# A gated linear attention with a PReLU network: the opening as one written sequence of small pieces, and state products ahead of off-diagonal ones

## The chip, the cores and the metric

The kernel runs on one core of one Trainium2 chip. Five engines run their own instruction streams and meet at semaphores: TensorE (PE; PEld is its weight load), VectorE (DVE), ScalarE (ACT), GpSimd (POOL) and SyncE (SP, which here only issues DMAs). The metric is the device time of one execution in microseconds, as the median over runs. All data are float32, but for the two weight matrices, which arrive as 64-bit floats and are turned into 32 bits on the chip.

## The reference

```python
# q, k, v, f_logit: (batch 4, heads 8, seq 768, dim 48)
f = 1.0 / (1.0 + np.exp(-f_logit))
for t in range(S):
    state = f[:, :, t, :, None] * state + np.einsum('bhd,bhe->bhde', k[:, :, t], v[:, :, t])
    y[:, :, t] = np.einsum('bhd,bhde->bhe', q[:, :, t], state)
x = y.transpose(0, 2, 1, 3).reshape(3072, 384)
h = x @ w_in                                   # w_in: 384 x 2048
g = np.maximum(h, 0.0) + alpha * np.minimum(h, 0.0)
out = g @ w_out                                # w_out: 2048 x 384
```

## The kernel before

The recurrence is cut into six chunks of 128 positions. A step is one chunk of two batch entries (eight heads each), so there are 12 steps: step n is the entry pair n % 2 and the chunk n // 2. Steps 0 and 1 have chunk 0, with an empty state and cheaper level products. Each step has four parts, written as generators that yield after a piece of work:

- `prepare` (P): loads of f, q, k, v (step 0 on SP's queue, the others on POOL's); the sigmoid and copies on ACT; on DVE the lagged products (L287 to L294), two scans (L317, L319), the level products (`us`) and the scaled queries and keys (`q3`, `kh`, `ks`); state queries copied into A (L419, ACT).
- `carry` (O): off-diagonal products `off` on PE (L444, and for chunk 0 the half products, L454) with ACT copies into A and `ad`; for chunk 0 the keys' transposes `pk`; then the state products `pd` (L484) and the first half of the state update, `moved(0)`.
- `attend` (S): for each of the two entries the scores `raw` (L520) and `qu` (L535) on PE, and masked copies of them into `ad` on DVE (L526, L541, L557); the diagonal blocks from `ad` to A (L563, eight copies, ACT); the outputs `py` (L574); `moved(1)`; the copy of `py` to `y` (ACT) and the change of layout to `xT`, in step 0 by products with `dense` (L592), later by ten DMAs on SP's, ACT's and POOL's queues.
- `network` (n): eight groups of the first layer `ph` (L618, six products of 256 columns), for each a Relu on ACT (L623) and two `gate` instructions on DVE (L625). The second layer is plain in step 0's network (`po`, L638), and in the others has seven half-size products in place of eight (L657), fed by sums of gates (L702) and of parts of w_out (L721).

The weights come in 16 pieces of 767 KB on SP's queue; ACT splits each (two instructions), and DVE combines them (L234). Piece f of w_in is what group f of step 0's network reads.

PE, DVE and ACT run in the order in which the program is written; a scheduler places POOL's and SP's instructions. That order is spelled out in letters, `FIRST` for the first four steps and `USUAL` for the others (Q is P of the next step, n the network of the step before). Ahead of all, 52 small products into a bank `idle` (L736) run on PE.

Of the kernel before, what the change touches and what calls it, by code (L numbers as in the profile page):

```python
# [17 lines left out]
C = 128  # L18
DB = 32
# [7 lines left out]
IDLE = 52  # L27
# [3 lines left out]
FIRST = (  # L31
        "P5 a2 P a O w S w a w a2 S Q S O S w Q2 S Q2 S w",
        "a2 w2 n O b w n b2 S P v2 n2 S b v Q n b n O S2 v n b v n Q2 b v Q b n S v2 W Q W S n2 W n",
        "n S P n2 S W n W n O Q n3 O S Q n S Q n Q S2 Q n3",
        "S n3 P S Q S n O n O n4 Q S Q S Q n S Q n Q n2",
)
USUAL = "S n2 S n2 O2 n Q n3 Q n Q S3 n Q S n Q n Q n"

def flat(first, usual, steps=12):
    out = []  # L40
    left = {}
    for n in range(steps + 1):
        for key in (first[n] if n < len(first) else usual).split():
            for _ in range(int(key[1:] or 1)):
                k = key[0]
                if k in "awbvW":
                    out.append((k,))
                else:
                    m = n - 1 if k == "n" else n + 1 if k == "Q" else n
                    k = "P" if k == "Q" else k  # L50
                    if 0 <= m < steps:
                        out.append((k, m))
    return out

# [4 lines left out]
def kernel(  # L59
# [12 lines left out]

# [31 lines left out]
    psn = ctx.enter_context(tc.tile_pool(name="psn", bufs=4, space=bass.MemoryType.PSUM))  # L120

    def pair(name):
        return psa.tile([128, 2, 512], F32, tag="pair", name=name)

    def bank(name):
        return psn.tile([128, 512], F32, tag="net", name=name)
# [35 lines left out]
    nc.gpsimd.memset(mquad, 0.0)  # L162
    for m in range(1, NB):
        lo = UO[m] + (4 if m == 1 else 0)
        n = NB - m
        nc.gpsimd.tensor_copy(mquad[:, lo:lo + 4 * n].rearrange("p (i r) -> p i r", r=4),
                              inq[:, 0:n].unsqueeze(2).broadcast_to((128, n, 4)))
    mhalf = const.tile([128, VW], F32, tag="mhalf", name="mhalf")
    nc.gpsimd.memset(mhalf, 0.0)
    for half in range(2):  # L170
        for m in range(1, NQ):
            n = NQ - m
            lo = 16 * half + 4 if m == 1 else VO[m] + 4 * n * half
            nc.gpsimd.tensor_copy(mhalf[:, lo:lo + 4 * n].rearrange("p (i r) -> p i r", r=4),
                                  inq[:, NQ * half:NQ * half + n].unsqueeze(2).broadcast_to((128, n, 4)))
# [7 lines left out]
    make_identity(nc, ident)  # L183
    nc.gpsimd.tensor_scalar(om, om, -1.0, 1.0, ALU.mult, ALU.add)


    dense = work.tile([128, DM], F32, tag="o", name="dense")
    nc.gpsimd.memset(dense, 0.0)
    for par in range(2):
        nc.gpsimd.tensor_copy(dense[:, (2 + par) * D:(3 + par) * D], ident[:, 64 * par:64 * par + D])  # L190

    def load_weights(dst, src, name):

        rows_ = NK if dst is w_in_sb else 1
        pieces_ = dst.shape[1] * dst.shape[2] // WP
        if rows_ == 1:
            dst = dst.rearrange("p a n -> p (a n)").unsqueeze(1)
        width = WP // rows_
        words = src.rearrange("p (a n) -> p a n", a=rows_).bitcast(I16)
        got = {}  # L210

        def of(n):
            return dst[:, :, n * width:(n + 1) * width]

        def by_row(t):
            return t.rearrange("p (a n) -> p a n", a=rows_)

        def upper(n):
            raw = stage.tile([128, WP, 4], I16, tag="raw", name=f"{name}_raw{n}", bufs=RAWS)
            nc.sync.dma_start(out=raw.rearrange("p (a n) four -> p a (n four)", a=rows_)[:, :, 0:4 * width - 1],  # L220
                              in_=words[:, :, 4 * n * width + 1:4 * (n + 1) * width])

            lead = stage.tile([128, WP], F16, tag="lead", name=f"{name}_lead{n}", bufs=LEADS)
            nc.scalar.activation(lead, raw[:, :, 2].bitcast(BF16), AF.Copy, scale=0.5)
            nc.scalar.activation(as_int(n, I32), by_row(raw.bitcast(U32)[:, :, 0]), AF.Copy, scale=2.0 ** -13)
            got[n] = lead

        def as_int(n, dtype):
            t = of(n).bitcast(dtype)
            return t if dtype is I32 else t.rearrange("p a (n two) -> p a n two", two=2)[:, :, :, 1]  # L230

        def both(n):
            t = by_row(got.pop(n).bitcast(I16))
            nc.vector.tensor_tensor(as_int(n, I16), as_int(n, I16), t, ALU.add)  # L234

        def uppers():
            for n in range(pieces_):
                upper(n)
                yield

        def rests():
            for n in range(pieces_):
                both(n)
                yield

        return uppers(), rests()
# [11 lines left out]
    def prepare(bp, c, x):  # L258

        i = f"{bp}_{c}"  # L260
        b0 = U * bp
        loads = nc.gpsimd if bp or c else nc.sync

        def load(name, src, bufs=2):
            t = work.tile([128, W], F32, tag=name, name=f"{name}_{i}", bufs=bufs)
            loads.dma_start(out=t.rearrange("p (u x) -> p u x", u=U),
                              in_=src[b0:b0 + U, c].rearrange("u p h t -> p u (h t)"))
            return t

        f = quads(load("f", fT, 1))  # L270
        q = load("q", qT, 1)
        k = x["k"] = load("k", kT, 1)

        for cc in range(NC2):
            t_, _ = halves(cc)
            loads.dma_start(out=vs[bp][t_, cc, :, 0:DM], in_=v[b0:b0 + U, c, t_].rearrange("u t d -> t u d"))


        nc.scalar.activation(f, f, AF.Sigmoid)
        nc.scalar.copy(kr[:, :, 2:3], f[:, :, 3:4])  # L280
        qdv = [qd[:, :, QO[d]:QO[d] + NB * (4 - d)].rearrange("p g (i r) -> p g i r", r=4 - d) for d in range(4)]
        nc.scalar.copy(qd[:, :, 0:DB], q.rearrange("p (g t) -> p g t", t=DB))  # L282
        fq = fs[:, 0:NS - 1].rearrange("p (g i) -> p g i", i=NB + 1)[:, :, 1:NB + 1]
        by32 = "p (g i) r -> p g (i r)"

        def lagged(d):
            nc.vector.tensor_tensor(qdv[d], qdv[d - 1][:, :, :, 1:5 - d],  # L287
                                    f[:, :, 1:5 - d].rearrange("p (g i) r -> p g i r", i=NB), ALU.mult)

        nc.vector.tensor_tensor(kr[:, :, 1:2], f[:, :, 2:3], f[:, :, 3:4], ALU.mult)  # L290
        lagged(1)
        nc.vector.tensor_tensor(kr[:, :, 0:1], f[:, :, 1:2], kr[:, :, 1:2], ALU.mult)
        lagged(2)
        nc.vector.tensor_tensor(fq, f[:, :, 0:1].rearrange(by32, i=NB), kr[:, :, 0:1].rearrange(by32, i=NB), ALU.mult)  # L294
        lagged(3)
        yield

        ps = work.tile([128, NS], F32, tag="ps", name=f"ps_{i}", bufs=1)  # L300
        ut = work.tile([128, G * UW], F32, tag="us", name=f"us_{i}", bufs=1)
        if c:
            us = ut.rearrange("p (g t) -> p g t", g=G)
        else:

            at = (0, VW, VW + 16, VW + 16 + DB, VW + 16 + DB + NB)
            us, q16, k16, g16 = (ut[:, G * lo:G * hi].rearrange("p (g t) -> p g t", g=G) for lo, hi in zip(at, at[1:]))
            nc.gpsimd.memset(k16[:, :, 16:DB], 0.0)
            nc.gpsimd.memset(g16[:, :, 3:5], 1.0)
            x["q16"], x["k16"] = q16, k16  # L310
        x["us"] = us
        q4 = us[:, :, 0:DB].rearrange("p g (i r) -> p g i r", r=4)
        for r in range(4):
            nc.scalar.copy(q4[:, :, :, r], qdv[r][:, :, :, 0])
        if not c:
            nc.scalar.copy(g16[:, :, 2:6:3], fq[:, :, 3:5])
        nc.vector.tensor_tensor_scan(ps, fs, ones, 0.0, ALU.mult, ALU.add)  # L317
        ss = work.tile([128, NS], F32, tag="ss", name=f"ss_{i}", bufs=1)
        nc.vector.tensor_tensor_scan(ss[:, ::-1], fs[:, ::-1], ones[:, ::-1], 0.0, ALU.mult, ALU.add)  # L319
        yield  # L320
        nc.vector.tensor_tensor(q4, q4, f[:, :, 0:1].rearrange("p (g i) o -> p g i o", i=NB)
                                .broadcast_to((128, G, NB, 4)), ALU.mult)
        pre = ps[:, 0:NS - 1].rearrange("p (g i) -> p g i", i=NB + 1)
        suf = ss[:, 1:NS].rearrange("p (g i) -> p g i", i=NB + 1)[:, :, 1:NB + 1]

        def earlier(m):

# [471 lines left out]
```

## Time and profile before

| What | Value |
|---|---|
| Median of 3 runs (lowest, highest) | 622.01 us (621.87, 624.6) |
| The profiled execution's span | 622.1 us |
| First network's first product | starts at 48.98 us |
| Step 4's first scores | start at 198.12 us |
| Step 5's first scores | start at 245.80 us |
| First copy of scores in step 4 on DVE | starts at 199.15 us |
| One L563 copy on ACT, 32 x 256 | 403 ns on average |
| One weight combination on DVE (L234) | 1.04 us |

Of a group of instructions the order of time gives the start, the busy time, the engine, the line, the operation, its operands as out<-in and their sizes, and in brackets how long the engine stood idle before it and on whom. A float32 product leaves two records in the trace. Instructions on one engine overlap a little, so the distance from start to start is shorter than the busy time of one. Busy time is not progress: a product can run at half its pace and count as busy.

### The profile page before, as it was taken

Reading aid. Unit: us, or ns where it says so; the run is one execution under the profiler, and the core shown is the slowest. Engines: PE = TensorE matmul, PEld = TensorE weight load, DVE = VectorE, ACT = ScalarE, POOL = GpSimd, SP = SyncE. Lnnn points to the kernel's source line nnn. Section 1 sums busy time; section 2 is a strip of 40 time slices with the busy share of each in tenths; the row PEclk is TensorE's granted clock in tenths of the full one; section 3 lists DMA queues with packets and bytes.
Section 4 is the critical chain, followed back from the end, with each engine's and each line's share of the span. In section 5 each row is a group of like instructions: output and inputs, shape, how many; then the busy total and the mean of one; then the engine's idle time right before and its main releaser. Section 6 shows DMA issues by size and latency. Waiting matters only on the chain.

```text
span 622.1 us, 19062 instructions
## 1 busy us (share of the span) xinstructions
PE 592.1 (95%) x8212; PEld 529.8 (85%) x8212; DVE 497.1 (80%) x997; ACT 246.6 (40%) x466; POOL 63.0 (10%) x117
## 2 busy tenths in 40 slices
PE   3568999999999999999999999999999999999997
PEld 3457866898899899899899899899889889889997
DVE  7588998899898798798798798798888888762261
ACT  5677862441641272262261351352253243223110
POOL 9120010001000011001001001001001000000000
PEclk9999999999999999999999999999999999999999
DMA  9964632014404314214313313413313401201000
GB/s 290 367 234 155 190 85 52 36 36 108 98 8 96 72 35 107 67 35 95 79 35 90 84 35 88 86 36 86 87 36 85 87 3 26 53 2 27 26 0 26
DMA packets 68116, 50.43 MB, mean 81 GB/s; under 512 B 47168, under 2 KB 60608, under 8 KB 68032
## 3 DMA queue, kind: packets, MB, share of 16 engines
q1 hardware_dynamic: 56656, 25.01, 15.6%
q0 software_dynamic: 6864, 22.35, 12.7%
q10 hardware_dynamic: 4512, 1.85, 1.7%
q8 instruction: 65, 1.06, 0.7%
q14 instruction: 19, 0.16, 0.1%
HBM read 36.21 MB, written 4.72 MB: 66 GB/s over the span
## 4 chain that ended last, share of the span: by engine, by line
PE 88%; DVE 6%; ACT 3%; issue 2%; DMA 1%; ACTq 0%; DVEq 0%
PE ph L618 39%; PE pc L657 9%; PE pa L657 8%; PE pd L657 5%; PE pe L657 4%; PE pb L657 4%; PE py L574 4%; PE po L638 3%; PE raw L520 3%; PE qu L535 3%; PE pd L484 3%; PE off L444 1%; PE xt L592 1%; DVE gate L625 1%; DMA f<-in_fT 1%
## 5 line engine op out<-in xcount | busy, mean ns | idle before, releaser
L618 PE MATMUL ph<-xT,w_in_sb 128*128 128x256 f32 x1152 | 258.7, 382 | 0.7 <-DVE Csum L661 0.7
L618 PEld LDWEIGHTS ph<-xT,w_in_sb 128*128 128x128 f32 x1152 | 216.4, 190 | 33.4 <-issue 2.3
L623 ACT ACTIVATE neg<-ph 128x512 f32<-128x512 f32 x96 | 57.4, 598 | 200.8 <-PE ph L618 139.5
L625 DVE SCALAR_TENSOR_TENSOR gate<-neg,om,ph 128x256 f32<-128x256 f32 x192 | 82.7, 478 | 50.6 <-ACT neg L623 50.4
L657 PE MATMUL pc<-t,S 128*128 128x192 f32 x352 | 61.7, 329 | 0.0
L657 PE MATMUL pa<-w_out_sb,gate 128*128 128x192 f32 x352 | 61.3, 327 | 0.1
L657 PEld LDWEIGHTS pa<-w_out_sb,gate 128*128 128x128 f32 x352 | 57.9, 190 | 1.0 <-DVE gate L625 0.4
L657 PEld LDWEIGHTS pc<-t,S 128*128 128x128 f32 x352 | 57.3, 190 | 0.6
L526 DVE COPY_PREDICATED ad<-mraw,raw 128x256 f32<-128x256 int32 (+1 forms) x96 | 42.4, 442 | 11.1 <-PE raw L520 8.6
L541 DVE COPY_PREDICATED ad<-mquad,qu 128x224 f32<-128x224 int32 (+6 forms) x140 | 42.0, 300 | 6.2
L419 ACT COPY A<-q 48x512 f32<-48x512 f32 x44 | 27.2, 619 | 36.1 <-DVE q L368 35.7
L563 ACT COPY A<-ad 32x256 f32<-32x256 f32 x96 | 38.7, 403 | 1.4
L330 DVE TENSOR_TENSOR us<-us,fs 128x768 f32<-128x768 f32 (+5 forms) x60 | 36.8, 614 | 0.0
L678 ACT ACTIVATE o<-pa 128x192 f32<-128x192 f32 x11 | 3.7, 332 | 75.2 <-PE pa L657 72.3
L661 DVE SCALAR_TENSOR_TENSOR Csum<-pc,Csum 128x192 f32<-128x192 f32 x22 | 7.9, 357 | 30.3 <-PE pc L657 30.1
L287 DVE TENSOR_TENSOR qd<-qd,f 128x768 f32<-128x768 f32 (+2 forms) x36 | 27.2, 756 | 6.0 <-ACT qd L282 6.0
L520 PEld LDWEIGHTS raw<-qd,k 48*32 48x32 f32 x1536 | 18.5, 109 | 15.3 <-issue 13.1
L520 PE MATMUL raw<-qd,k 48*32 48x80 f32 x1536 | 24.0, 243 | 7.6 <-issue 4.4
L702 DVE TENSOR_TENSOR S<-gate 128x512 f32<-128x512 f32 x44 | 30.3, 688 | 0.8
L657 PE MATMUL pe<-w_out_sb,S 128*128 128x192 f32 x176 | 30.4, 326 | 0.0
L657 PE MATMUL pd<-w_out_sb,S 128*128 128x192 f32 x176 | 30.4, 326 | 0.0
L657 PE MATMUL pb<-t,gate 128*128 128x192 f32 x176 | 30.4, 326 | 0.0
(101 smaller groups left out, 758.3 us busy)
## 6 DMA issues: line engine op xcount, KB each, us to landing
w_out_raw<-in_w_out SPq DMA_DIRECT2D x8, 767.8 KB, 5.8
w_in_raw<-in_w_in SPq DMA_DIRECT2D x8, 767.2 KB, 11.9
q<-in_qT POOLq DMA_DIRECT2D x11, 512.0 KB, 4.2
f<-in_fT POOLq DMA_DIRECT2D x11, 512.0 KB, 4.5
k<-in_kT POOLq DMA_DIRECT2D x11, 512.0 KB, 4.9
out<-o SPq DMA_DIRECT2D x24, 192.0 KB, 2.7
vs<-in_v POOLq DMA_DIRECT2D x22, 192.0 KB, 4.6
ksn<-kt SPq DMA_DIRECT2D x80, 32.0 KB, 2.0
```

The lines of the kernel that those rows point to most:

```text
L287: nc.vector.tensor_tensor(qdv[d], qdv[d - 1][:, :, :, 1:5 - d], f[:, :, 1:5 - d].rearrange("p (g i) r -> p g i r", i=NB), ALU.mult)
L330: nc.vector.tensor_tensor(us[:, :, UO[m]:UO[m] + 4 * n].rearrange("p g (i r) -> p g i r", r=4), us[:, :, skip:skip + 4 * n].rearrange("p g ...
L419: nc.scalar.copy(A[halves(cc)[1], :, par * HP:(par + 1) * HP, CH * cc:CH * (cc + 1)], q3[rows(par)].rearrange("p (u h c) s t -> p u h c (s ...
L520: nc.tensor.matmul(raw[DB * j:DB * (j + 1), par, hp * C:hp * C + QW], lhsT=k[r_, g * DB:(g + 1) * DB], rhs=qd[r_, g], start=True, stop=True)
L526: nc.vector.copy_predicated(adu[:, :, :, d:4], mraw[:, d, :, d:4].bitcast(I32).unsqueeze(1).broadcast_to((128, H, NB, n)), rv[:, :, QO[d]: ...
L541: nc.vector.copy_predicated(ad[:, u, :, :, 4 * m:DB], mquad[:, lo:lo + n].bitcast(I32).unsqueeze(1).unsqueeze(1).broadcast_to((128, 2, HP, ...
L563: nc.scalar.copy(A[s_, u, :, s_], ad[s_, u].rearrange("p r h t -> p (r h) t"))
L618: nc.tensor.matmul(ph[:, j * T:(j + 1) * T], lhsT=w_in_sb[:, kt, m * 128:(m + 1) * 128], rhs=xT[:, kt], start=(kt == 0 and j == 0), stop=( ...
L623: nc.scalar.activation(neg, phv, AF.Relu, scale=-1.0)
L625: nc.vector.scalar_tensor_tensor(gate[:, m % NH, m // NH], neg[:, j], om[:, m:m + 1], phv[:, j], ALU.mult, ALU.add)
L657: nc.tensor.matmul(to[:, 0:DH], lhsT=of(f), rhs=by(f), start=(f == 0 and not more), stop=(f == NH - 1), skip_group_check=True)
L702: nc.vector.tensor_tensor(to, x_, y_, op)
```

## The change

The generators become named words. Each word is one small piece (one weight load, one copy, one group of products), bound to a step; `FIRST` is now one sequence of 455 words over the first four steps, and `USUAL` one of 98 words for a later step. What changes beside the cut:

- The 52 idle products and their bank are gone. During step 0 the four banks of the networks' pool serve as a second pool of pairs (`psf`).
- POOL's instructions run in written order too. Most of POOL's constants now stand in one word, C, which comes after the first loads and ahead of the blank columns of step 0 (`bl`).
- In the first four steps some copies move: of the diagonal blocks (`p`), 19 go to POOL and five to DVE; the state queries of steps 0 and 1 (`s`) go to POOL; one copy of `py` in steps 0 and 3 goes to DVE.
- In chunk 0 the half products go into free columns of the scores' pair, right behind the scores, with one ACT copy for each entry; `qu` has one pair for both entries; the scores come before the keys' transposes and the off-diagonal products.
- In step 0 the layout products run in two halves of 128 columns, one for each entry, each behind the copy of its `y`.
- Weight pieces are loaded in another order, and ACT's two instructions and DVE's one for a piece are words of their own, some a good deal apart.
- In every later step the state products and the first half of the state update come before the off-diagonal products. Some DVE products change places within their stage.
- The second layer is plain for n < PLAIN with PLAIN = 1, which is step 0's network, as before.

```diff
-IDLE = 52
+PLAIN = 1
+FIRST = """
+ld:0 C:0 bl:0 ld:1 id1:0 id7:0 id0:0 id2:0 id3:0 sg:0 qc:0 c0:0 kr:0 l1:0 l2:0 l3:0 k4:0 c2:0 cg:0 c1:0 c3:0 r1:0 r0:0 le:0 gk:0 h0:0 h1:0 H0:0 ih1:0
+il0:0 il7:0 il1:0 ih7:0 ih0:0 H1:0 il3:0 sc:0 ke:0 kp:0 kc:0 sg:1 fs:0 sa:0 nr:0 x1:0 x0:0 R0:0 sb:0 X0:0 ib1:0 R1:0 X1:0 ib0:0 of:0 oc1:0 oc0:0 qc:1
+l1:1 p13V:0 s10:0 p00G:0 bl:1 s11:0 p02G:0 p03G:0 p01G:0 p12G:0 p11G:0 pd:0 m0:0 y0:0 z0V:0 p10G:0 y1:0 ld:2 ib7:0 l2:1 l3:1 m1:0 kr:1 ih3:0 ih2:0
+il2:0 z1A:0 t0:0 T00A:0 T01A:0 T02A:0 t1:0 c1:1 T10A:0 T11A:0 ib3:0 jd0:0 id6:0 id5:0 id4:0 c0:1 T12A:0 n0:0 c2:1 c3:1 il5:0 cg:1 il6:0 ih6:0 n1:0
...
-USUAL = "S n2 S n2 O2 n Q n3 Q n Q S3 n Q S n Q n Q n"
+USUAL = """
+r0 R0 x0 X0 n0- g0- G0- n1- g1- G1- r1 R1 x1 X1 n2- g2- G2- n3- g3- G3- S0- pd m0 of oc0 oc1 n4- g4- G4- ld+ sg+ kr+ qc+ l1+ l2+ l3+ c0+ c1+ c2+ c3+
...
+        def states(cc, par):
+            copy = nc.scalar.copy if c else nc.gpsimd.tensor_copy
...
+        def put(u, j, engine):
+            s_ = slice(DB * j, DB * (j + 1))
+            copy = {"A": nc.scalar.copy, "V": nc.vector.tensor_copy, "G": nc.gpsimd.tensor_copy}[engine]
+            copy(A[s_, u, :, s_], ad[s_, u].rearrange("p r h t -> p (r h) t"))
...
-    idle = bank("idle")
...
-    with tc.manual_schedule(engines={mybir.EngineType.PE, mybir.EngineType.DVE, mybir.EngineType.Activation}):
-        for _ in range(IDLE):
-            nc.tensor.matmul(idle[0:32, 0:8], lhsT=ones[:, 0:32], rhs=ones[:, 0:8], start=True, stop=True)
+    with tc.manual_schedule(engines={mybir.EngineType.PE, mybir.EngineType.DVE, mybir.EngineType.Activation, mybir.EngineType.Pool}):
...
+        for name, step in ORDER:
+            (pieces[name] if name in pieces else run[step, name])()
```

A word's number behind the colon is its step (in `USUAL`, a minus means the step before, a plus the next). `ld` loads; `sg`, `qc`, `kr`, `c` are ACT's preparation, `l`, `le`, `k4`, `gk`, `nr`, `sc`, `ke`, `sa`, `sb`, `fs` DVE's; `r` scores, `R` their copies, `x` quad scores, `X` theirs, `h`/`H` half products and copies; `kp`/`kc` key transposes and copies; `of`/`oc` off-diagonal, `pd` state products, `m` state update; `s`, `p` copies into A; `y` outputs, `z` their copies, `t`/`T` layout products and copies, `mv` layout DMAs; `n`, `g`, `G` a group of the first layer, its Relu and gates; `v` an eighth of the plain second layer; `id`, `ih`, `il`, `ib` a piece of w_in (load, two ACT parts, DVE), `j` the same of w_out.

## The prediction

> **What bounds the kernel now.** I read the page's busy shares first, then the table of stretches, then the order of time of the opening. TensorE (PE) is the bound, but not everywhere:
>
> ```profile
> PE 592.1 (95%) x8212; PEld 529.8 (85%) x8212; DVE 497.1 (80%) x997; ACT 246.6 (40%) x466; POOL 63.0 (10%) x117
> PE   3568999999999999999999999999999999999997
> ...
> 0.00:10.00 10.00, 5.72 (x104) 5.62 (x104) 6.11 (x8) 5.66 (x7) 8.57 (x31) 1.00 0.83 238
> 10.00:20.00 10.00, 1.66 (x127) 1.55 (x130) 10.00 (x20) 4.41 (x7) 7.21 (x12) 1.00 1.05 386
> 20.00:30.00 10.00, 5.74 (x259) 4.83 (x251) 3.55 (x9) 8.58 (x16) 0.00 (x0) 1.00 1.05 355
> 30.00:40.00 10.00, 5.70 (x208) 4.87 (x193) 8.34 (x17) 8.13 (x15) 2.15 (x4) 1.00 0.93 344
> 40.00:50.00 10.00, 8.29 (x53) 6.91 (x52) 10.00 (x19) 5.06 (x12) 1.94 (x3) 1.00 0.32 95
> 200.00:600.00 400.00, 399.20 (x5214) 363.00 (x5215) 319.03 (x660) 140.50 (x276) 29.70 (x47) 1.00 0.25 57
> ```
>
> The columns of a stretch are its length, then PE, PEld, DVE, ACT, POOL busy. From 200 to 600 us PE is busy for 399.2 of 400 us, so no reordering there can win more than 0.8 us. In the first 50 us PE has 27.1 us of records, and 5.7 of these are the 52 idle products. There the time is to be had. The order of time shows how the opening hangs together:
>
> ```profile
> 7.44 3.24 POOL L174 COPY mhalf<-inq 128x12 f32<-128x12 f32 x6
> 14.29 0.21 POOL L309 MEMSET us<- 128x64 f32 x1
> 17.79 1.08 PE L444 MATMUL off<-q,kh 48*32 48x32 f32 x64 [9.96 <-DVE q L368]
> 27.46 1.87 DVE L526 COPY_PREDICATED ad<-mraw,raw 128x256 f32<-128x256 int32 x4 [6.16 <-PE raw L520]
> 35.66 1.00 DVE L557 COPY_PREDICATED ad<-mhalf,qu 128x224 f32<-128x224 int32 x3
> 43.73 5.46 PE L592 MATMUL xt<-y,dense 128*128 128x256 f32 x12 [1.71 <-ACT y L583]
> 48.98 3.15 PE L618 MATMUL ph<-xT,w_in_sb 128*128 128x256 f32 x12
> ```
>
> First number: start; second: busy. PE waits 10 us for step 0's preparation, then DVE waits 6.2 us for the first scores, the last masked copies end at 36.7, and the first network begins at 49.0. From there to step 4's first scores (198.1) PE has few gaps; after that come 424.0 us of which the change touches only an order.
>
> **The change, part by part.** I follow step 0 down the new order with start-to-start times of the rows (a DVE product of 1024 columns 1.13, of 512 columns 0.60; four L526 copies 1.9; three L557 copies 0.95; one weight combination 0.94).
>
> (a) Step 0's preparation. f is ready at 5.8 as before. q's copy on ACT now stands ahead of f's, so the second DVE product starts at 6.9, not 7.5, and the three lags end at 10.0. k4 and the level products follow, to 12.3, two short products to 12.7. Then DVE needs k16's blank columns. Before, Pool wrote them between its constants (done 14.5); now they stand behind all of them, the same instructions, so about 14.4: a stall of 1.7. k16 and q16 1.2, scans 1.35, keys 1.8, factors 0.35, starts 0.6, near products 1.0: 20.7. The scores need only the lags, so PE runs both from 10.0, and the 6.2 us wait of DVE is gone. Copies 1.9 (22.6), starts 0.7, quad copies 1.0 (24.3), a weight 0.94, copies 1.9 and 0.9: 28.0. Before this point was 36.7, so 8.7 earlier.
>
> (b) From there to the first network, 12.3 us before (36.7 to 49.0). The diagonal copies move from ACT (0.40 each) to Pool, which has done no copy of 256 columns. Below: Pool's memsets give 0.18 us and 0.8 ns a column, so 0.4. Above: the two 48-column copies of dense took 2.19 together, 1.1 each where their 0.2 was expected, so 0.9 of waiting: 1.3. I take 0.8 (the six mhalf copies, 0.54 for 0.19, are the nearer rows), and 1.1 for a 512-column state copy. One state copy from 23.3, a diagonal one from 24.3, the next blanks 0.75, a state and three diagonal copies: 29.3; the other three, 31.7. Then the second half of the outputs, 1.9 as before (33.6), with the layout's first half behind it. The layout keeps its price as two halves, 5.46, at the slow pace of its row (0.91 a product of 256 columns, where L618 has 0.45): 39.0. Last copies and start: **40.0**, 9.0 earlier than before. With both ends of Pool's price, and layout products at 0.45: 36.5 to 44.
>
> SP sends five weight pieces first (1, 7, 0, 2, 3; five buffers), and the sixth when ACT has freed one. ACT has the key copies behind piece 3: 2.0 MB of inputs and 3.8 MB of pieces, at the 238 and 386 GB/s of the first two stretches, are in at about 19, or 24 if step 1's loads share the way; the keys are then copied by 26 and the first state by 29.5, in time for the outputs at 29.3. Were they 5 us later still, so would be the network. Pieces 4 to 6 come a few us after ACT frees their buffers (about 22) and are wanted from 46.
>
> The idle products cost nothing to remove: 10 us of waiting came behind them, and the transposes at 20.8 ran at 0.25 us, twice the 0.136 of those at 54.9.
>
> The Trainium skill ("TensorE: Matmul & The Clock Gate", Part 1) says that the clock falls to half after an idle window of about 3.4 us and returns after as long a busy one. The trace agrees in the products' pace (0.91 against 0.45), though its clock column reads 1.00 throughout. By that rule a new opening dense enough to be warm would have the layout for 2.7 instead of 5.4.
>
> (c) From the first network to the end of step 1's outputs. Before, 49.0 to 86.9, with two of the eight parts of the second layer; now with one, so 84.3 on the old clock (a part is 2.63). In the new order: two groups of the first layer at 5.4 together; DVE's level product waits for ACT's last column copies behind the layout copies (38.6 to 41.2, a new stall of 2.6), the first score copies of step 1 wait for ACT's half copy, which stands behind weight pieces (to 52.4, 1.1), and DVE ends the last quad copies at 69.1. Four diagonal and two state copies on Pool follow, 5.4: 74.5. PE is through with the part at 71.3, waits 3.2, and ends the outputs at 76.4. That is 7.9 ahead of 84.3, so 1.1 of the 9.0 is lost.
>
> (d) To step 4. DVE's instructions ahead of its first score copy of step 4 sum to 174.0 us, before 171.1 (the added ones are copies of y and A taken over from ACT). Before, that copy began at 199.2, so DVE had 28 us of idle time; 7.9 earlier leaves 17.3. By step 2's k4 (74.6 on my chain, 64.3 in the sum) 10.3 are spent, so 7.0 are left; before, DVE idled for 8.2 after 75 us, mostly waiting for PE's groups. That nearly closes: I add nothing, and keep 0 to 7 for the range.
>
> (e) Later steps. State products (0.9) now go ahead of the off-diagonal ones (0.7). What comes behind both, four groups of 2.7, covers the copies into A; the state update has its operand 0.7 earlier. In the eight steps no wait of PE stands there: 0, from -0.8 to 0.8. Pool is now in a written order, with the next loads behind the output moves. Step 5's f would be issued once step 3's moves are out (about 190), and is wanted after the fifth group of step 4 (about 219): 0, and nothing else stands in that queue.
>
> Sum: 622.1 (the profiled span, 0.1 from the median of 622.0, so no correction) - 9.0 + 1.1 = **614 us**.
>
> **The rivals.**
> 1. *DVE becomes the bound of the opening.* For it: only 7 us of slack by (d). Against it: DVE's waits for PE vanish when DVE is late. If the 8.2 us of waits stay (1.2 over the slack) and Pool's 23 copies hold DVE for half of their 0.4 us each (4.6), 5.8 is lost: 620, hardly a change.
> 2. *Pool's copies are slow (the slower side).* Each lies directly in front of output products. At 1.3 for a diagonal copy and 1.5 for a state copy, step 0's seven and two add 4.3, step 1's four and two 2.8, steps 2 and 3, seven diagonal, 3.5; each also holds DVE for 0.4, and 23 x 0.4 is 9.2, of which DVE's slack takes 7. 614 + 10.6 + 2.2 = 627. It decides from about 1.2 us a copy. For it: the mhalf and dense rows, which ran beside two-input DVE products. Against it: half of the copies run beside L526 and L557, which take one operand from PSUM. The Trainium skill ("SBUF — State Buffer", Who interferes with whom) has this as a rule: a DVE instruction with two SBUF inputs and a GpSimd one that reads SBUF block each other whole. The trace agrees for Pool's side (0.54 against 0.14 to 0.2 in the mquad copies, 1.00 for seven); it shows no DVE instruction made longer.
> 3. *Everything goes through at the low ends*: Pool at 0.4, the layout warm: 36.5 instead of 40.0, no wait in step 1: 622.1 - 12.5 - 2.0 = 608.
> 4. *The change does less than it says*: the first network could start early and find its weights late. Against it: the pieces 1 and 0 are combined at 25.2 and 29.0 on my chain, 10 us ahead.
>
> **How the numbers follow.** 614 gets 0.60, rival 1 0.16, rival 2 0.12, rival 3 0.10, rival 4 (no change, 622) 0.02. The range goes from 606 to 621: it takes in rivals 1 and 3 and the ends of (b), and leaves out rival 2. About 0.5% (3.1 us) is what a measurement here can tell from no change. Faster than 618.9: the forecast, rival 3 and part of rival 1, 0.76; within: 0.12; slower: 0.12.
>
> **What would show it.** Right: step 0's quad copies end near 28, the first network starts near 40, step 4's scores near 190, and the steps stay at 47.7 us (198.1 to 245.8 before). Wrong: Pool copies over 1 us; outputs of steps 0 to 3 that wait for Pool; DVE without idle time from 40 to 190 while PE waits for it; a first network later than 45.

## The result and the profile after

The changed kernel takes 640.55 us (median of four runs, 636.31 to 644.2), the kernel before beside it 621.94: 1.029 times as long (95% interval 1.023 to 1.034). The forecast was 614, with a range of 606 to 621: wrong in sign and outside the range. The profiled execution took 638.74, its span is 637.0 against 622.1, so 14.9 us are to be found:

| Stretch | before | after | difference |
|---|---|---|---|
| Start to the first network | 48.98 | 43.66 | -5.3 |
| First network to step 4's first scores | 149.14 | 154.99 | +5.9 |
| Step 4's to step 11's first scores (seven steps) | 333.90 | 349.15 | +15.3 |
| From there to the end | 90.1 | 89.2 | -0.9 |

So two things went wrong: the opening gained nothing up to step 4 (198.65 against 198.12, where some 8 were expected), and the later steps, of which nothing was expected, lost 15.3. The page after, shares and granted clock:

```profile
PE 591.7 (93%) x8120; PEld 528.0 (83%) x8120; DVE 502.4 (79%) x1004; ACT 236.2 (37%) x439; POOL 77.3 (12%) x140
...
PEclk9999899999999899999999999999989979999999
```

Before, the row of clocks was 9 throughout. PE is busy for as long as before (591.7 against 592.1, of which 5.7 were the idle products), in a span longer by 14.9: it now waits, and for some time it runs at a lower clock. The order of time of the opening after (start, busy, engine and line, in brackets the idle time before and whom it waited for):

```profile
10.70 2.40 PE L459 MATMUL raw<-qd,k 48*32 48x80 f32 x128 [10.70 <-DVE qd L307]
...
18.13 0.45 PE L518 MATMUL raw<-ut 48*32 48x16 f32 x34 [1.36 <-issue]
...
21.00 1.38 PE L480 MATMUL qu<-ut,k 48*32 48x52 f32 x86 [0.21 <-DVE ut L307]
28.11 0.84 PE L480 MATMUL qu<-ut,k 48*32 48x52 f32 x42 [5.73 <-issue]
...
33.18 1.19 PE L575 MATMUL state<-vs,ksn 64*48 64x48 f32 x43 [2.77 <-issue]
...
43.66 7.94 PE L682 MATMUL ph<-xT,w_in_sb 128*128 128x256 f32 x36
...
64.85 0.33 PE L480 MATMUL qu<-ut,k 48*32 48x52 f32 x2 [4.47 <-issue]
65.11 7.45 PE L682 MATMUL ph<-xT,w_in_sb 128*128 128x256 f32 x24
```

The scores start at 10.7, close to the 10.0 of the forecast. But PE then stops four times in the middle of a run of small products, on no other engine ("issue"): 1.36, 5.73, 2.77 and 4.47. Behind the last one 24 products of the first layer take 7.45, elsewhere 5.45. The table of stretches says why (length; PE, PEld, DVE, ACT, POOL busy; granted clock, DMA share, GB/s):

```profile
60.00:62.00 2.00, 0.38 (x32) 0.23 (x28) 2.00 (x5) 1.20 (x3) 1.41 (x3) 1.00 0.93 329
62.00:64.00 2.00, 0.00 (x0) 0.00 (x0) 2.00 (x5) 0.00 (x0) 0.00 (x0) 0.59 0.96 325
64.00:66.00 2.00, 1.15 (x4) 0.93 (x4) 1.16 (x4) 0.00 (x0) 0.00 (x0) 0.50 1.04 307
66.00:68.00 2.00, 2.00 (x6) 1.55 (x6) 0.00 (x0) 0.00 (x0) 0.00 (x0) 0.50 0.47 121
```

The clock falls while PE stands and stays at half until 68; the DMA engines are full until 66. Of the later steps, the list of PE's waits from 198 us to the end (total, times, longest) and the order of time in step 5 and step 10:

```profile
PE state L575 <- DMA ksn<-kt: 5.1, 8, 1.5
PE off L553 <- issue: 2.2, 1, 2.2
PE ph L682 <- issue: 1.6, 1, 1.6
PE state L575 <- issue: 0.9, 2, 0.7
```

```profile
263.35 0.28 PE L575 MATMUL state<-vs,ksn 64*48 64x48 f32 x2
263.87 0.26 PE L575 MATMUL state<-vs,ksn 64*48 64x48 f32 x2 [0.23 <-issue]
264.34 1.12 PE L575 MATMUL state<-vs,ksn 64*48 64x48 f32 x60 [0.22 <-DMA ksn<-kt]
265.39 0.76 PE L553 MATMUL off<-q,kh 48*32 48x32 f32 x64
...
509.94 0.89 PE L575 MATMUL state<-vs,ksn 64*48 64x48 f32 x58 [0.59 <-DMA ksn<-kt]
510.75 0.71 PE L553 MATMUL off<-q,kh 48*32 48x32 f32 x59
513.63 0.32 PE L553 MATMUL off<-q,kh 48*32 48x32 f32 x5 [2.18 <-issue]
513.88 13.51 PE L682 MATMUL ph<-xT,w_in_sb 128*128 128x256 f32 x48
```

Before, that list was empty. Now the state products wait for the sixteen small moves of the keys (`ksn` from `kt`), which had never held anybody up. These waits sum to 9.8. The products of the first layer show another part: the 48 behind the wait in step 10 take 13.51, where before they took 10.63, with the clock at 0.50 from 514 to 518. Over the span `ph` sums to 266.3, against 260.2 in a run below (e3) without the waits on the keys: 6.1 more.

### The profile page after: what moved, and what is told of

Same layout as the page of the kernel before. It is cut to its first block, busy times and chain, and to the rows that moved or that the text cites. A ratio compares the mean times of both kernels' runs of the same rounds, so it can differ in the third digit from the quotient of the medians.

```text
span 637.0 us, 18839 instructions
## 1 busy us (share of the span) xinstructions
PE 591.7 (93%) x8120; PEld 528.0 (83%) x8120; DVE 502.4 (79%) x1004; ACT 236.2 (37%) x439; POOL 77.3 (12%) x140
## 3 DMA queue, kind: packets, MB, share of 16 engines
q8 instruction: 64, 1.05, 0.7%
## 4 chain that ended last, share of the span: by engine, by line
PE 63%; SPq 9%; DMA 9%; DVE 9%; issue 5%; POOL 2%; ACTq 2%; ACT 1%; DVEq 0%; POOLq 0%
PE ph L682 30%; SPq L436 9%; PE pa L752 7%; PE pc L752 5%; DMA ksn<-kt 5%; PE py L613 4%; PE pb L752 4%; DMA xT<-y 4%; PE pe L752 2%; PE pd L752 2%; PE state L575 2%; PE po L712 2%; ACTq L650 2%; PE qu L480 1%; PE off L553 1%
## 5 line engine op out<-in xcount | busy, mean ns | idle before, releaser
L682 PE MATMUL ph<-xT,w_in_sb 128*128 128x256 f32 x1152 | 266.3, 390 | 1.6 <-issue 1.6
L682 PEld LDWEIGHTS ph<-xT,w_in_sb 128*128 128x128 f32 x1152 | 221.5, 195 | 36.1 <-issue 3.5
L650 POOL DMA_DIRECT2D xT<-y x22 | 11.9, 544 | 268.3 <-ACT y L622 268.3
L307 DVE TENSOR_TENSOR ut<-ut,fs 128x256 f32<-128x256 f32 (+3 forms) x70 | 40.4, 580 | 0.7
L418 ACT COPY A<-q 48x512 f32<-48x512 f32 x40 | 24.7, 617 | 43.4 <-DVE q L307 43.1
L326 ACT COPY ut<-qd 128x256 f32<-128x256 f32 x48 | 30.6, 669 | 14.9 <-DVE qd L307 9.2
L480 PE MATMUL qu<-ut,k 48*32 48x112 f32 (+1 forms) x1536 | 26.0, 258 | 10.4 <-issue 10.2
L459 PE MATMUL raw<-qd,k 48*32 48x80 f32 x1536 | 22.4, 243 | 10.7 <-DVE qd L307 10.7
L599 ACT COPY A<-ad 32x256 f32<-32x256 f32 x72 | 28.6, 400 | 9.0 <-DVE ad L488 7.9
L613 PEld LDWEIGHTS py<-A,vs 128*64 128x64 f32 x768 | 25.7, 145 | 7.2 <-issue 3.7
L613 PE MATMUL py<-A,vs 128*64 128x64 f32 x768 | 28.0, 233 | 3.6 <-POOL A L418 2.1
```

The source lines that it names most:

```text
L307: nc.vector.tensor_tensor(a, b, of, ALU.mult)
L326: w[f"c{r}"] = lambda r=r: nc.scalar.copy(q4()[:, :, :, r], qdv[r][:, :, :, 0])
L459: nc.tensor.matmul(to[DB * j:DB * (j + 1), par, hp * C:hp * C + QW], lhsT=x["k"][r_, g * DB:(g + 1) * DB], rhs=qd[r_, g], start=True, stop ...
L480: nc.tensor.matmul(to[DB * j:DB * (j + 1), par, o + 4:o + width], lhsT=x["k4"][r_, g * DB:(g + 1) * DB], rhs=x["us"]()[r_, g, 4:width], st ...
L613: nc.tensor.matmul(to[64 * par:64 * par + 64, u, o:o + CH], lhsT=vs[bp][:, cc, u, hd * D:hd * D + 64], rhs=A[:, u, par * HP + hp, CH * cc: ...
L682: nc.tensor.matmul(ph[f][:, j * T:(j + 1) * T], lhsT=w_in_sb[:, kt, m * 128:(m + 1) * 128], rhs=x["T"][:, kt], start=(kt == 0 and j == 0), ...
```

## The experiments

The first idea on the later steps (theory B in the expectations): the state products read what the key moves bring, the off-diagonal ones don't; ahead of them they meet the landing, so the new order on PE is the cause. On the opening (theory A): "issue" is PE without instructions, which are late while the weights' transfers fill the DMA engines. All runs, with the stretch from step 4's to step 11's first scores in the profiled execution:

| Run | median us | ratio to before (95%) | step 4 at | seven steps |
|---|---|---|---|---|
| before | 621.3 to 622.0 | | 198.12 | 333.9 |
| after | 640.55 | 1.029 (1.023 to 1.034) | 198.65 | 349.2 |
| e1 | 630.92 | 1.015 (1.011 to 1.019) | 200.90 | 338.2 |
| e2 | 616.87 | 0.992 (0.989 to 0.994) | 198.74 | 329.8 |
| e3 | 621.28 | 0.999 (0.997 to 1.001) | 200.51 | 329.9 |
| e4 | 628.13 | 1.009 (1.005 to 1.012) | 193.88 | 340.2 |
| e5 | 622.94 | 1.002 (1.001 to 1.003) | 199.78 | 332.8 |
| e6 | 623.85 | 1.005 (1.002 to 1.007) | 196.05 | 334.8 |
| e7 | 629.96 | 1.014 (1.011 to 1.017) | 194.41 | 343.5 |
| e8 | 619.81 | 0.997 (0.995 to 0.999) | 196.21 | 332.4 |
| e9 | 616.83 | 0.994 (0.991 to 0.996) | 197.98 | 329.5 |
| e10 | 615.46 | 0.991 (0.989 to 0.992) | 196.46 | 329.4 |
| e11 | 622.04 | 1.002 (1.000 to 1.003) | 199.91 | 330.0 |
| e12 | 615.39 | 0.989 (0.986 to 0.992) | 192.16 | 329.9 |

The two columns on the right come from one execution each: e10's profiled one was its longest (616.78), e12's its shortest (612.97), so a few us between two rows of "step 4 at" show nothing by themselves.

**e1, the changed kernel with the off-diagonal products ahead again.**

```diff
-... S0- pd m0 of oc0 oc1 n4- ...
+... S0- of oc0 oc1 pd m0 n4- ...
```

> The changed kernel with one thing put back: in the later steps the off-diagonal products come ahead of the state products again; the first four steps stay as changed. Theory B (what was lost in the later steps is PE's wait for the landing of the key moves, and the half clock that follows it): from the first scores of step 4 on the steps are 47.7 us long again, 334 for the seven in place of 349, step 4's scores stay near 198.6, and the time is 622 to 624. Rival (the finer order of ScalarE's, VectorE's and Pool's pieces costs the time, whatever the order on PE): the steps stay 48 to 53 long and the time stays above 632.

It came between the two: 630.92. Half of the loss goes, half stays, and the state products still wait, although they come later (3.5 us in five steps, in four of them for the key moves, in one by the list for an output's move on the same queue).

**e2, the kernel before with the state products ahead from step 4 on.**

```diff
+        if c >= 2:
+            states()
+            yield
+            offs()
+            yield
+            return
         offs()
```

> The kernel before with one thing taken from the change: from step 4 on the state products and the first move of the state come ahead of the off-diagonal products. Theory B: PE waits for the key moves' landing, the clock falls behind the wait and six or more of the groups of eight tiles at that place take 12 us and more in place of 10.6; the time is 633 to 640. Rival (the order alone is harmless, the finer pieces did it): 620 to 624.

Theory B falls: 616.87, 5.1 *faster* than before. The order of time of its step 5, and that of the kernel before:

```profile
259.82 1.06 PE L477 MATMUL pd<-vs,ksn 64*48 64x48 f32 x64
260.80 0.76 PE L445 MATMUL off<-q,kh 48*32 48x32 f32 x64
261.49 10.63 PE L630 MATMUL ph<-xT,w_in_sb 128*128 128x256 f32 x48
```

```profile
260.08 0.76 PE L444 MATMUL off<-q,kh 48*32 48x32 f32 x64
260.92 1.58 PE L484 MATMUL pd<-vs,ksn 64*48 64x48 f32 x64
262.43 10.63 PE L618 MATMUL ph<-xT,w_in_sb 128*128 128x256 f32 x48
```

Ahead, the state products wait for nothing and take 0.94 to 1.06; in the kernel before, directly behind the off-diagonal ones they take 1.58, in all eight steps. Start to start the two groups take 1.67 instead of 2.35 in this step, so 0.68; eight times that is 5.4. The new order on PE is a gain, if the keys are there. In this step SP issues its last key move 10.9 us behind the first scores, and nothing waits for it.

**e3, the changed kernel with every other key move issued by Pool.**

```diff
-                    nc.sync.dma_start(
+                    (nc.gpsimd if b % 2 and n >= FROM else nc.sync).dma_start(
```

> The changed kernel, state products still ahead, but every other one of the sixteen key moves of a step from step 4 on is issued by Pool instead of all by SP. Theory B: the last key move lands some 4 to 5 us earlier, the state products wait for nothing, the groups behind them take 10.6 us, and the time is 617 to 624. Rival (the order itself lowers the clock, or the wait is another one): 634 to 642.

As theory B had it: in step 5 SP issues its last key move 4.6 us behind the first scores, in the changed kernel 11.0; from there on no product waits for a key move (one wait of 0.58 stands in step 2, which the edit leaves as it was); the steps are 47.0, but for the last of the seven. So the late landing is the cause, and the order only exposes it. Beside e3 the changed kernel loses 19.3 in the seven steps, more than the 15.3 beside the kernel before, since the order's own gain is in the 15.3: its state groups take 10.4 longer from their start to that of the off-diagonal ones, and the rest is mostly the first layer at half clock and the two waits on "issue" (1.6 and 2.2). The issue itself is not late: 11.0 is hardly more than the 10.9 of e2. What made the landing late? The order of time on Pool, before and after:

```profile
254.28 0.73 POOL L266 DMA_DIRECT2D k<-in_kT  x1 [18.52 <-PE raw L520]
...
280.76 0.61 POOL L276 DMA_DIRECT2D vs<-in_v  x1
...
301.93 0.73 POOL L266 DMA_DIRECT2D k<-in_kT  x1 [18.49 <-PE raw L520]
```

```profile
257.57 0.72 POOL L295 DMA_DIRECT2D k<-in_kT  x1 [17.61 <-PE raw L459]
258.29 1.21 POOL L299 DMA_DIRECT2D vs<-in_v  x2
```

Before, the scheduler had each step's v loaded some 20 us ahead of its k, around the output moves; only k's 512 KB came while key moves were under way. Pool's written order has both parts of v right behind k, so 384 KB more at that time. Pool's loads are queue q0, the moves are on q1 (packets, MB, share of the 16 engines); stretches of 2 us, after from 257.5 and before from 254:

```profile
q0 software_dynamic: 16, 0.07, 48.1%
q1 hardware_dynamic: 544, 0.05, 21.8%
...
q0 software_dynamic: 166, 0.62, 76.6%
...
q1 hardware_dynamic: 944, 0.23, 61.6%
q0 software_dynamic: 90, 0.23, 49.3%
```

```profile
q1 hardware_dynamic: 544, 0.05, 19.2%
q0 software_dynamic: 4, 0.02, 8.4%
...
q0 software_dynamic: 132, 0.49, 66.6%
q1 hardware_dynamic: 385, 0.02, 13.0%
...
q1 hardware_dynamic: 575, 0.22, 40.7%
q0 software_dynamic: 8, 0.02, 2.6%
```

After, not one packet of q1 moves from 259.5 to 261.5; the last key moves come through between 261.5 and 263.5, while the state products start at 263.35 and stand until 264.34. Before, 385 packets got through beside k's load and the rest was done by 260. A 16 KB move takes 1.9 us to land without such loads; beside k's load some took up to 5.2 before, and beside k's and v's up to 6.2 after. The Trainium skill ("DMA: Bandwidth & Descriptors", Queues, rings and completion order) says that each DMA engine takes turns between its queues, a whole packet at a time, and that a packet is typically 9 to 17 descriptors. In these 2 us the 16 engines move 166 of what the profile calls packets, some ten each, all of q0. That fits one such turn if the profile's packets are the page's descriptors, which no run here shows. That is theory C: it is v's loads. e5, e6 and e7 test it.

**e4, the weights' transfers cut down** (as e1, but pieces behind the fifth reuse the five buffers' contents).

```diff
+            if len(held) == RAWS:
+                raws[n] = held[turn[0] % RAWS]
+                turn[0] += 1
+                return
```

> As the run with the off-diagonal products ahead, and only the first five pieces of the weights are loaded; the later pieces are cast from the same five buffers again, so the transfers of the other pieces are left out and the networks work with wrong weights. Theory A (the opening's stalls of PE that end with its own issue are instructions that come late, because the weights' transfers fill the DMA engines): the stalls of 5.7 us at 22 to 28 and of 2.8 at 30 to 33 shrink to under 1.5 each, that of 4.5 at 60 to 65 goes with the half clock behind it; the first network starts at 37 to 40, step 1's outputs end at 73 to 78, and the time is 609 to 614. Rival (the stalls don't come from the transfers): the stalls stay and the time is that of the run with the off-diagonal products ahead.

Beside e1 the stalls are 4.95, 1.67 and 1.52 in place of 5.76, 3.59 and 4.91, and step 4 starts 7.0 us earlier. So the transfers make the stalls longer, but do not alone make them: 1.67 is left with the DMA engines at 0.03 of full or less from 26 to 32. The 4.95, where the rule said under 1.5, says less: the first five pieces and the inputs keep the engines full until 24 there too. The total (628) missed the 609 to 614, mostly since e1 itself, its base, was not the 622 that was expected.

**e5, v's loads late** (their own word `lv` behind the output moves `mv`; state products ahead, moves all on SP).

```diff
-z1A mv A2- C2- ...
+z1A mv lv+ A2- C2- ...
```

> The changed kernel, state products still ahead, key moves still all on SP; only the two loads of the next step's v stand in Pool's queue behind this step's output moves (where they came in the kernel before), no longer directly behind the load of k. Theory C (Pool's written order puts v's loads into the microseconds in which the last key moves have to land): from step 4 on the state products wait for nothing, take 0.94, the steps are 46.9 to 47.1 long, and the time is 617 to 623. Rival (k's load alone, or the queue of sixteen moves, makes the landing late): waits of 0.5 and more at the state products, steps of 48 and more, time 630 and more.

622.94, 1.4 above its own runs of the kernel before: some 17 of the 18.6 lost are back with two DMA issues of a step moved. Behind k's load alone the small moves now stand still for 0.5 us (no packet of q1 from 258.5 to 259.0). From step 6 on the steps are 47.0; the first two and the last are 48.2, with 0.65 of waiting for the keys in step 4 and 1.09 of "issue" in step 10, so the expected time held, and the expected steps four times in seven.

**e6 and e7, the kernel before with Pool in written order**, alone and together with e2's order:

```diff
-    with tc.manual_schedule(engines={..., mybir.EngineType.Activation}):
+    with tc.manual_schedule(engines={..., mybir.EngineType.Activation, mybir.EngineType.Pool}):
```

> The kernel before with one thing taken from the change: Pool's instructions in the written order (so f, q, k, v, v of the next step follow each other); the off-diagonal products stay ahead of the state products. Theory C: from step 4 on v's loads follow k's, the last key moves land 5 to 6 us after their issue, the state products wait 0.5 to 0.9 behind the off-diagonal ones in most steps, the steps are 48.2 to 48.7, and the time is 626 to 632. Rival (Pool's order costs nothing by itself): steps of 47.7, 621 to 624.

> The kernel before with both: Pool's instructions in the written order and, from step 4 on, the state products ahead of the off-diagonal ones. Theory C: the wait falls on the state products before the off-diagonal ones can cover it, the steps are 48 to 51 long as in the changed kernel, and the time is 633 to 641, 16 to 24 above the run with the state products ahead alone. Rival (the two don't act on each other): the sum of the single ones, about 621 to 627.

In the seven steps: before 333.9, order of PE alone 329.8 (-4.1), Pool's order alone 334.8 (+0.9), both 343.5 (+9.6, where the two singles sum to -3.2). The medians say the same: -5.1, +2.3 and +8.4. Both times came out lower than expected, but the interaction is what theory C says: off-diagonal products ahead cover most of a late landing, and state products ahead meet it. The changed kernel loses 5.6 more in these steps than e7; nothing here separates that.

**e8, e5 with step 1's quad products behind one more group of the first layer.**

```diff
-r0:1 h0:1 x0:1 jl1:0 jh0:0 jh4:0 g6:0 qc:2 H0:1 n2:0 ...
+r0:1 h0:1 jl1:0 jh0:0 jh4:0 g6:0 qc:2 H0:1 n2:0 x0:1 ...
```

> As the run with v's loads late, and in the opening the quad products of step 1 (x0:1) go behind one more group of the first layer (n2:0), so that 192 small products (384 instructions with their weight loads) no longer stand in one piece. Theory A (PE's stalls in the opening are instructions that come in blocks of 256 and come late under full DMA engines): the stall of 4.5 to 4.9 at 60 to 66 falls under 2 and the half clock behind it goes; step 4's first scores come 3 to 6 us earlier than in the run with v's loads late, and the time is 612 to 618. Rival (a block that comes late stalls PE wherever it stands, since the transfers and not the density of the products decide): the stall moves and the time is that of the run with v's loads late.

The stall at 60 to 66 falls to 2.04, step 4 starts 3.6 earlier than in e5, and the time falls by 3.1, a little less than expected (619.81).

**e9, e8 with the moves of e3; e10, and step 1's k and v loaded later; e11, and three weight buffers in place of five.**

```diff
-RAWS, LEADS = 5, 4
+RAWS, LEADS = 3, 4
...
-p10G:0 y1:0 ld:2 ...
+p10G:0 lk:1 y1:0 ld:2 ...
```

(`lk:1` loads k and v of step 1; the first pair of lines belongs to e11 alone.)

> The run with v's loads late and the quad products of step 1 split, and every other key move from step 4 on is issued by Pool: the two remedies of the later steps together. Theory C: the two steps after step 4's scores, 47.7 each in that run, become 47.0 too; the time is 617 to 619. Rival (Pool's longer queue delays the other loads): 620 and more.

> As the three edits together, and step 1's k and v (0.9 of the 1.9 MB of its inputs) are loaded behind Pool's copies of step 0's diagonal (about 36) and not at 15.5. Theory A (a block of 256 instructions is asked for when the one before is entered, and comes after 4 us with free DMA engines, later with full ones): the full stretch ends some 2 us earlier, the stall of 5.7 at 22 shrinks by 1 to 3, that of 2.8 at 30 goes down to 1.7; the first network starts 2 to 4 us earlier than at 44.2 and the time is 1 to 4 less than with the three edits. Rival (the stall is of fixed length or belongs to the products): no change of the stalls, the time as with the three edits.

> As the run with step 1's k and v later, and only three pieces of the weights are under way at once instead of five (three buffers; the last column copy of piece 3 goes behind step 0's off-diagonal copies on ScalarE). Theory A: the DMA engines are free from about 14 to 20, when the block for the quad products is asked for, so the stall at 22 falls under 2; the first network starts at 38 to 41 and the time is 612 to 616, if the weights come in time. Rival 1 (weights late): PE waits for the first network's weights after 45, and the time is that of the three edits or more. Rival 2 (stalls not from the transfers): the stall stays at 5.7.

e9 is as expected but for 0.2 us (616.83; both early steps 47.0). In e10 the big stall falls from 5.47 to 4.11 and the next from 4.14 to 1.94: 615.46, faster than both kernels. In e11 the DMA share from 10 to 20 falls from 1.05 to 0.81 (0.73 and 0.57 behind 14) and the stall stays at 4.09: theory A's "under 2" is wrong: less load ahead of the stall did not shorten it. From 22 to 26, while PE stands, the engines are full again (1.03), so what the load does during the stall is not separated here. The weights come late there, which was its first rival: ScalarE waits 4.0 and 1.6 for pieces between 49 and 61, PE then 4.5 for a gate behind them, and the gain is lost.

**e12, e10 with 30 idle products ahead of the first scores.** In all runs with this opening the stalls stand at the same product, and 128 products apart: 34 + 8 + 86 from the first to the second, 42 + 64 + 21 = 127 to the third. With their weight loads that is 256 instructions.

```diff
+            for _ in range(0 if n or not u else 30):
+                nc.tensor.matmul(to[0:32, 0, 0:8], lhsT=ones[:, 0:32], rhs=ones[:, 0:8], start=True, stop=True)
```

> As the run with step 1's k and v later, and 30 idle products (60 records of PE with as many weight loads) stand ahead of step 0's first scores, while PE waits there anyway; their results are written over. Theory A in the form of the runs so far (PE's instructions come in blocks of 256, that is 128 products with their weight loads; where small products use one up in under 2.5 us, PE stands until the next is there): all borders move up by 60 products. The stalls that stood behind 94 products of the short scores, 86 of the quad products and 21 of the state products stand behind 34, 26 and, 60 products earlier than 21 state products, 25 of the off-diagonal ones (24 to 26); their lengths stay 0.5 to 1.4, 4.1 and 1.9, each within 1 us, and the time stays within 2 us of 615.5. Rival (the stalls belong to the kind of product or to a transfer at that time): they stay behind 86 of the quad products and 21 of the state products.

The order of time of its opening:

```profile
15.60 0.47 PE L533 MATMUL raw<-ut 48*32 48x16 f32 x34 [2.57 <-DVE ut L320]
16.90 1.11 PE L533 MATMUL raw<-ut 48*32 48x16 f32 x94 [0.83 <-issue]
...
20.94 0.58 PE L495 MATMUL qu<-ut,k 48*32 48x52 f32 x26 [0.22 <-DVE ut L320]
23.25 1.54 PE L495 MATMUL qu<-ut,k 48*32 48x52 f32 x102 [1.72 <-issue]
25.39 0.58 PE L568 MATMUL off<-q,kh 48*32 48x32 f32 x25 [0.60 <-ACT ksn L551]
29.87 0.76 PE L568 MATMUL off<-q,kh 48*32 48x32 f32 x39 [3.90 <-issue]
```

The stalls moved to 34, 26 and 25 products, to the product as the count says: that sets their place. Their lengths did not keep to the expectation (1.72 and 3.90, where 4.1 and 1.9 were expected). The stall of 2.9 in step 1's quad products is gone too; its border now falls in the first layer (0.38), and one of 1.6 stands in step 1's state products instead. The time is that of e10.

## Why the prediction was wrong

(a) *Step 0's preparation.* Scores at 10.7 (10.0), and the first entry's near copies done at 22.6, as forecast. Then the step fails: the quad copies end at 33.7, not 28.0, as DVE waits 5.75 for the quad products behind the stall of 5.73; the 2.77 comes behind them, in the state products. The sum had DVE's and Pool's times but took PE's small products at the pace of their rows. The trace of before had stalls at the same two counts: 350 and 477 product records from the start, in either kernel.

```profile
26.67 0.56 PE L520 MATMUL raw<-qd,k 48*32 48x80 f32 x17 [1.10 <-issue]
...
32.81 0.61 PE L520 MATMUL raw<-qd,k 48*32 48x80 f32 x18 [2.29 <-issue]
```

DVE waited 6.16 and 1.35 for the scores behind them; the prediction put the first of these waits down to the order alone. Packed denser, the stall at 350 grew to 5.73 and became the path.

(b) *To the first network.* The prices were right or high: Pool's first diagonal copy 1.03, the next six 0.70 each (0.8 was taken), state copies 0.60 (1.1), layout 3.85 (5.46, or 2.7 at the fast pace). 43.66 in place of 40.0 is (a)'s delay less these. Rival 2, slow Pool copies, falls, though its sign came true: a copy took 0.39 beside a `gate` (75.69) and 1.03 beside a weight combination (30.12), which fits a slowing by DVE, but the mean of step 0's seven is 0.75, far from the 1.2 at which the rival was to decide.

(c) *To the end of step 1's outputs.* 85.3, not 76.4: 3.7 brought along, 4.47 of stall, 2.0 of half clock behind it, less 1.1 as Pool's wait was 2.1 and not 3.2; together 9.0, where 8.9 was missed.

(d) *To step 4.* Right: 113.35 from there, 113.8 before on the same count. The forecast of 190 for step 4 failed by (a) and (c) alone. In e10 the issue stalls still sum to 9.5, more than the 6.5 by which its step 4 misses 190.

(e) *Later steps: "In the eight steps no wait of PE stands there: 0, from -0.8 to 0.8", and on Pool's order, "nothing else stands in that queue".* This is the step that cost the sign. No wait stood there before; the question was what stands there once the order is changed. Three rows of before answered it: the last key move was issued at 256.2 with products on them 4.7 us later, k's load was issued at 254.3, and v's far from it, at 280.8 and 282.8. The prediction followed f's load through the new queue, not v's. The gain was missed as well: `pd` at 1.58 in the later steps and 0.94 in step 3, where it stood alone (168.38). So "no reordering there can win more than 0.8 us", read from 399.2 of 400 us busy, was wrong: e2 wins 4.1 in seven steps by order alone, since the 1.58 counts as busy.

No rival held either mechanism: three weighed engines against each other, and rival 4 thought of late transfers, but of the weights only. Both losses are at transfers (the keys' moves, and the blocks of PE's instructions) that cost little as long as less was packed around them.

## What to carry to other kernels

When a queue goes from a scheduler's order to a written one, list each DMA's issue time before and after, and what is in flight when a small transfer must land: two loads moved by some 20 us cost more than the whole reordering could win. Put consumers of a late transfer ahead only when the transfer has time to spare. Runs of hundreds of small products are to be counted in blocks of instructions, and broken up by big ones.

## What the runs showed of the hardware

- PE's instructions come in blocks of 256, and a run of small products uses one up in 1.4 to 2.4 us (128 products with their loads: 1.43 before at 19.4, 2.40 after at 10.7). At the border PE then stands, up to 6.0 us in these runs, longer under full DMA engines (e1 against e4: 3.59 and 1.67 at the same place). What else sets the length stays open (e4's 4.95, e11's 4.09, e12's two). The Trainium skill ("Runtime: NRT & Kernel Launch", Instruction fetch mechanics) gives the blocks as 16 KB or 256 instructions on a DMA queue of their own and calls the cost of a border mostly hidden. The trace agrees with the size (16240 products and weight loads of the changed kernel are 63.4 blocks, and the instruction queue shows 64 packets, 1.05 MB; before, 64.2 and 65) and not with the cost. In e1 a packet of that queue passes at 25.4, inside the stall, and PE goes on at 28.0.
- The granted clock fell to half within 2 us of a short pause: behind waits of 0.59 and 2.18 in step 10 it is 0.73, then 0.50 from 514 to 518. The Trainium skill ("TensorE: Matmul & The Clock Gate", Part 1) sets the idle window at about 3.4 us; here less was enough, with only small products around it. Not each short pause did it: behind 1.64 in step 5 the clock stays at 1.00.
- The same 64 state products take 1.58 directly behind the off-diagonal ones and 0.94 ahead of them. Why was not tried.
